# The second piece of the first batch's keys and values asked for on ScalarE's queue

## The chip, the core and the metric

The kernel runs on one core of a Trainium2 chip. The metric is the device time of one launch in microseconds (us). The core's engines are TensorE (PE in the profile; PEld is its weight load), VectorE (DVE), ScalarE (ACT), GpSimd (POOL) and SyncE (SP). SyncE computes nothing here: it issues most of the loads, in the order in which they are written. ScalarE and GpSimd can issue loads and stores too, each on a queue of its own; in the profile SyncE's queue is q1, ScalarE's q10 and GpSimd's q0.

## The reference

Eight batches of eight heads, 576 tokens each, head size 64, 32 slots. The attention goes over slots into which keys and values are summed, and its output goes through a mixture of eight experts, of which each token takes one.

```python
a = exp(phi - max); a = a / (sum + 1e-9)
k_m = einsum('bhsm,bhsd->bhmd', a, k)          # keys and values summed into 32 slots
v_m = einsum('bhsm,bhsd->bhmd', a, v)
attn = softmax(q @ k_m.T / sqrt(64))
x = (attn @ v_m)                               # as 4608 tokens of 512 features
idx = argmax(norm(x) @ norm(emb).T / tau)      # the token's expert
out = gate * (relu(x @ w1[idx]) @ w2[idx])
```

## The kernel before

The eight batches are worked one after the other. For each, the kernel picks one expert, loads that expert's w1 and w2 and computes the whole batch with it; tokens that chose another are noted in flags and worked by a branch at the end if there are any. For the first batch the expert is picked early, from the summed values of the slots, before the attention is done (`summed`, `guess`, `pick`).

The order of every engine's instructions is the order in which the code is written, since the kernel asks for a manual schedule. Waits are put in by semaphores. A load that is issued has landed when its semaphore is full.

The start of the kernel, which the change touches, goes like this. Filler products (`warm`) run on TensorE while nothing else is there. SyncE issues phi of batch 0 in two pieces (tile `ex`), then `load_kv(0)`: keys and values of 512 tokens in two pieces of 1024 KB, `kx[0]` and `kx[1]`, with those of the last 64 tokens (`kl`, 256 KB) between them. Then comes half of q (`qt`). ScalarE issues two small loads for the router (`em`, `tv`), and runs one small exp, which loads its table. The softmax of phi (`softmax`, `largest`), its transposes (`turn`, `tails`) and the sums into slots (`slots`, tiles `acc0t` and `acc0m`) follow. `slots` is called three times for batch 0: with `kx[0]`, then with `kl`, then with `kx[1]`, with three filler products (`hot`) after each of the first two. Behind it stand the scaled sums (`ks`), the keys (`tk`), the pick of the expert, and, on SyncE, the load of the pick's number and the loads of w1 (`load_w1`, in two halves for this batch).

The second batch's keys and values go into the same tiles: `load_kv(1, (0,))` and two calls of `load_piece`, each of which waits until the products that read the tile before are done. The second batch's `slots` runs in five parts, and before the last of them TensorE multiplies the first batch's values with the first half of w1 (`project`, tile `pg`). From the products `ph` on (`first`) TensorE's work is one long row.

Of the kernel before, what the change touches and what calls it, by code (L numbers as in the profile page):

```python
# [307 lines left out]
class Kernel:  # L308
# [156 lines left out]
    def load_kv(self, b, ks=range(2)):  # L465
        if 1 < b < B:
            for g in range(NG):
                to, x = self.kl[64 * g : 64 * g + 64], self.kvt[b, :, 4 * g : 4 * g + 4]
                self.nc.sync.dma_start(to, x)
        if b < B:  # L470
            for k in ks:
                self.nc.sync.dma_start(self.kx[k], self.kv[b, :, 2 * k : 2 * k + 2])
                if b < 2 and not k:
                    x = self.kvt[b].rearrange("t (g j) d -> (t g) (j d)", g=NG)
                    self.nc.sync.dma_start(self.kl.rearrange("p j d -> p (j d)"), x)
# [634 lines left out]
@with_exitstack  # L1110
def moe_linformer(ctx, tc, phiT, qT, kv, kvt, emb, tau, w1, w2, out):
    k = Kernel(ctx, tc, phiT, qT, kv, kvt, emb, tau, w1, w2, out)
    ctx.enter_context(tc.manual_schedule(engines={ET.PE, ET.DVE, ET.Activation, ET.SP, ET.Pool}))


    k.eights()
    k.warm(11)
    k.warm(5, hot=k.mm([P, 64], "cool", 0))
    k.load_phi(0)
    k.load_kv(0)  # L1120
    k.load_q(0, (0,))
    k.load_router()
    k.consts()
    accs = [k.ps.tile([P, 2 * D], F32, tag=f"{n}3", name=f"acc0{n}", bufs=1) for n in "tm"]
    for vT in k.vT:
        k.nc.vector.memset(vT, 0.0)
    router = k.router()
    for g in range(NG):
        k.largest(0, g)
        k.softmax(0, (g,))  # L1130
    for g in range(NG):
        k.turn(0, g)
        if not g:
            next(router)
        k.warm(4 if g else 8, hot=k.mm([P, 256], f"half{g}", 0))
    k.tails(0)
    k.shares(0)
    next(router)
    k.load_phi(1, (0,))
    k.load_q(0, (1,))  # L1140
    k.load_phi(1, (1,))
    t = Tokens(k, 0, k.pt)
    for ks in ((0, 1), (4,), (2, 3)):
        k.slots(0, accs, ks=ks, first=0 in ks, last=3 in ks)
        if 3 not in ks:
            k.warm(3, hot=k.mm([P, 128], f"hot{ks[0]}", 0))
    k.scale(0)
    next(router, None)
    k.warm(2, hot=k.mm([P, 128], "hot2", 0))
    k.load_kv(1, (0,))  # L1150
    k.load_piece(1, 2)
    k.keys(0)
    t.summed()
    k.again()
    values = k.values(0, copy=k.nc.scalar.copy, room=lambda *a: k.mm(*a, 3))
    all, tr, te = slice(0, BL), [k.mm([P, S - 64], f"tr0_{g}", g) for g in range(NG)], [k.mm([P, 64], "te0_0", 2)]
    k.score(0, tr, 64, S, (0,))
    t.guess()
    k.score(0, te, 0, 64, (0,))
    next(values)  # L1160
    t.fill((0,), slice(2, BL), tr)
    e = t.pick()
    t.fill((0,), slice(0, 2), te)
    list(values)
    k.load_w1(e, 0)
    k.load_piece(1, 3)
    k.load_w1(e, 1)
    k.load_q(1, (0,))
    tl = [k.pt([P, D + E], f"tl0_{g}") for g in range(NG)]
    k.squares(0, tl)  # L1170
    k.score(0, tr, 64, S, (1,))
    te.append(k.pt([P, 64], "te0_1"))
    k.score(0, te, 0, 64, (1,))
    k.products(0, copy=True)
    work = [t.weigh((g,), all, None if g else k.nc.gpsimd) for g in range(NG)]
    next(work[0])
    for g in range(NG):
        k.largest(1, g)
    next(work[0])
    t.fill((1,), slice(2, BL), tr)  # L1180
    t.fill((1,), slice(0, 2), te)
    k.softmax(1, (0,))
    list(work[0])
    k.softmax(1, (1,))
    k.warm(12, hot=k.mm([P, 256], "warm0", 3))
    k.turn(1, 0)
    for _ in range(2):
        next(work[1])
    k.warm(9, hot=k.mm([P, 128], "warm1", 3))
    k.turn(1, 1)  # L1190
    list(work[1])
    k.tails(1)
    k.shares(1, v=k.nc.gpsimd, invert=False)
    project = k.project(0, k.vT[0], apart=True)
    accs = [accs[0], k.mm([P, 2 * D], "acc1", 3)]
    for ks in ((0,), (1,), (4,), (2,), (3,)):
        if 3 in ks:
            next(project)
        k.slots(1, accs, ks=ks, first=0 in ks, last=3 in ks)
    next(project)  # L1200
    t.divide(range(NG), all, True, lambda: k.invert(1))
    k.tags, k.turns = 4, 3
    k.scale(1)
    k.again(k.nc.scalar.copy)
    t.turn(range(NG), all)
    for g in range(NG):
        k.part(g, slice(0, HS), k.nc.gpsimd.tensor_copy)
    next(project)

    def between():  # L1210
        k.keys(1, lambda *a: k.mm(*a, 3))
        list(k.values(1, copy=k.nc.scalar.copy, room=lambda *a: k.mm(*a, 2)))

    t.attend(between)
    t.turned(0, 1)
    t.turned(4)
    k.load_w2(e)
    k.load_q(1, (1,))
    k.load_phi(2)
    k.second_part = project  # L1220
    for b in range(B):
        u = Tokens(k, b + 1, k.pt) if b < B - 1 else None
        left = k.batch(b, t, u)
        t = u
    k.rest(*left)
# [29 lines left out]
```

## Time and profile before

| what | us |
| --- | --- |
| median of three runs | 393.88 |
| the three runs | 391.99, 393.88, 394.16 |
| the profiled execution | 392.9 |
| its span, from the first to the last instruction | 391.1 |
| TensorE busy in the span | 382.4 |

The profiled execution is 1.0 us under the median; 1.8 us of it lie outside the span. Times in the rows are microseconds from the span's start. In a row of the timeline the two numbers at the front are start and length, x16 is a count of merged instructions, and the brackets at the end tell how long the engine was idle before, and what ended that. "SPq" and "ACTq" are the issues of loads, not the transfers. A transfer's time is told by the view of the DMA issues, as the time from the issue to the landing.

### The profile page before, as it was taken

What the parts mean: (1) busy time and instruction counts of PE and PEld (TensorE: products, weight loads), DVE (VectorE), ACT (ScalarE), POOL (GpSimd) and SP (SyncE); (2) the same over time, 40 slices, a digit from 0 to 9 for tenths busy, and PEclk for the clock granted to TensorE, in tenths of its full rate; (3) what the DMA queues carried; (4) which work ended last, traced back from release to release, by engine and by line L of the source; (5) the groups of instructions that cost most, each with busy time, mean ns of one, the idle gap of its engine ahead of it and who ended that gap; (6) DMA issues with size and microseconds to landing.
All of it is one profiled execution on the core that took longest, in us unless ns stands there. A gap on an engine that the chain in (4) does not pass through costs nothing. (4 is left out here: it accounts for less than half of the span.)

```text
span 391.1 us, 10317 instructions
## 1 busy us (share of the span) xinstructions
PE 382.4 (98%) x3847; PEld 311.6 (80%) x3847; DVE 243.2 (62%) x800; ACT 213.4 (55%) x665; POOL 190.3 (49%) x234
## 2 busy tenths in 40 slices
PE   8979999999999999999999999999999999999995
PEld 5658878799787978889787987879788897879883
DVE  5668896679673798259862798538861596535000
ACT  5446734778484875666656675657641751145011
POOL 1156940596154932479061951559242871529300
PEclk9999999999999999999999999999999999999999
DMA  8999828993789936995499916996369306890011
GB/s 317 399 370 353 340 63 220 373 398 130 164 272 376 403 80 140 390 392 205 90 286 371 407 38 142 332 393 244 71 180 369 137 2 122 263 370 1 30 54 44
DMA packets 65590, 91.23 MB, mean 233 GB/s; under 512 B 40728, under 2 KB 45336, under 8 KB 63488
## 3 DMA queue, kind: packets, MB, share of 16 engines
q1 hardware_dynamic: 62160, 81.02, 61.2%
q0 software_dynamic: 2688, 8.26, 5.8%
q10 hardware_dynamic: 688, 1.26, 1.2%
q8 instruction: 31, 0.51, 0.5%
q14 instruction: 23, 0.19, 0.1%
HBM read 71.19 MB, written 19.33 MB: 231 GB/s over the span
## 5 line engine op out<-in xcount | busy, mean ns | idle before, releaser
L791 PE MATMUL ph<-aT,gh 128*128 128x288 f32 x512 | 103.1, 296 | 0.0
L831 PE MATMUL py<-wh,hh 128*128 128x512 f32 x256 | 100.9, 394 | 0.0
L831 PE MATMUL py<-wl,hh 128*128 128x512 f32 x256 | 99.8, 390 | 0.0
L831 PE MATMUL py<-wh,hl 128*128 128x512 f32 x256 | 99.7, 389 | 0.0
L756 POOL TENSOR_TENSOR wl<-w2s,wh 128x512 fp32r<-128x512 f32 x64 | 83.2, 1301 | 5.1
L791 PEld LDWEIGHTS ph<-aT,gh 128*128 128x128 f32 x512 | 81.8, 188 | 1.8 <-DVE hl L798 0.8
L791 PE MATMUL ph<-aT,gl 128*128 128x288 f32 x256 | 75.4, 294 | 0.0
L795 ACT ACTIVATE hh<-ph 128x224 fp32r<-128x224 f32 (+1 forms) x128 | 48.8, 388 | 33.5 <-PE ph L791 33.0
L798 DVE SCALAR_TENSOR_TENSOR hl<-ph,hh 128x224 fp32r<-128x224 f32 (+1 forms) x128 | 51.8, 417 | 23.7 <-ACT hh L795 17.2
L997 POOL DMA_DIRECT2D out_dram<-ys x28 | 16.3, 582 | 91.1 <-ACT ys L836 91.0
L836 ACT ACTIVATE ys<-py,gate 128x512 f32<-128x512 f32 (+1 forms) x40 | 25.7, 643 | 63.6 <-PE py L831 33.8
L831 PEld LDWEIGHTS py<-wh,hh 128*128 128x128 f32 x256 | 48.1, 188 | 11.1 <-issue 1.4
L831 PEld LDWEIGHTS py<-wh,hl 128*128 128x128 f32 x256 | 48.1, 188 | 10.2
L831 PEld LDWEIGHTS py<-wl,hh 128*128 128x128 f32 x256 | 48.1, 188 | 9.5
L791 PEld LDWEIGHTS ph<-aT,gl 128*128 128x128 f32 x256 | 48.0, 188 | 0.0
L775 DVE TENSOR_TENSOR gl<-pg,gh 128x512 fp32r<-128x512 f32 x32 | 20.0, 684 | 42.9 <-ACT gh L771 42.9
L755 POOL CAST wh<-w2s 128x512 fp32r<-128x512 f32 x62 | 41.3, 666 | 0.3 <-DMA w2s<-w 0.3
L746 POOL TENSOR_TENSOR aT<-aw,aT 128x576 fp32r<-128x576 f32 (+1 forms) x18 | 23.5, 1320 | 35.0 <-DVE aT L745 29.2
L584 ACT COPY eT<-xt 32x256 f32<-32x256 f32 x80 | 32.3, 404 | 1.4
L820 PE MATMUL py<-w2s,h 128*64 128x256 f32 x256 | 29.4, 382 | 0.0
L656 ACT COPY kv<-kt 32x64 f32<-32x64 f32 x96 | 23.3, 243 | 6.3 <-DVE kt L646 5.1
L820 PEld LDWEIGHTS py<-w2s,h 128*64 128x64 f32 x256 | 17.7, 137 | 10.7 <-DVE aw L102 2.1
(184 smaller groups left out, 471.6 us busy)
## 6 DMA issues: line engine op xcount, KB each, us to landing
kx<-kv SPq DMA_DIRECT2D x15, 1024.0 KB, 11.8
w2s<-w SPq DMA_DIRECT2D x28, 512.0 KB, 9.9
w1s<-w SPq DMA_DIRECT2D x28, 512.0 KB, 6.6
qt<-qT SPq DMA_DIRECT2D x14, 576.0 KB, 9.7
out_dram<-ys POOLq DMA_DIRECT2D x28, 256.0 KB, 6.5
ad<-aw SPq DMA_DIRECT2D x8, 576.0 KB, 11.5
td<-x SPq DMA_DIRECT2D x56, 72.0 KB, 2.3
ea<-td SPq DMA_DIRECT2D x7, 512.0 KB, 4.4
```

Of the source, the lines that this page charges most:

```text
L584: nc.scalar.copy(eT[to, :8, m].rearrange("p (g k) m -> p g k m", g=NG), xt[at, :, q : BL - 2 : 4])
L656: nc.scalar.copy(y, self.kt[32 * l : 32 * l + 32, g, h + 2 * i :: 2 - 4 * i])
L746: self.nc.gpsimd.tensor_tensor(out=al, in0=a, in1=ah.bitcast(F32), op=ALU.subtract)
L755: (copy or self.nc.scalar.copy)(h, x)
L756: self.nc.gpsimd.tensor_tensor(out=l, in0=x, in1=h.bitcast(F32), op=ALU.subtract)
L775: nc.vector.tensor_tensor(out=self.gl[:, g, f], in0=ps[g], in1=self.gh[:, g, f].bitcast(F32), op=ALU.subtract)
L791: nc.tensor.matmul(p, lhsT=w[:, g, fs], rhs=x[:, g, to], start=g == 0 and k == 0, stop=g == 1 and k == 2)
L795: nc.scalar.activation(self.hh[:, f, at], q, AF.Relu)
L798: nc.vector.scalar_tensor_tensor(out=self.hl[:, f, at], in0=q, scalar=0.0, in1=self.hh[:, f, at].bitcast(F32), op0=ALU.max, op1=ALU.subtract)
L820: nc.tensor.matmul(p[64 * j : 64 * j + 64], lhsT=self.h4[:, f], rhs=self.w2s[:, f, d * j : d * j + d], start=f == 0, stop=f == 7,)
L831: nc.tensor.matmul(p, lhsT=h[:, f, to], rhs=w[:, f], start=f == 0 and k == 0, stop=f == 7 and k == 2)
L836: nc.scalar.activation(y[:, :d], p, AF.Copy, scale=gate[:, i : i + 1])
```

## The change

`load_kv` for batch 0 is split into two calls. The first asks for `kx[0]` and `kl` on SyncE, as before. The second, which asks for `kx[1]`, is written behind `load_router`, and issues on ScalarE. For the other batches nothing is different.

```diff
         if b < B:
             for k in ks:
-                self.nc.sync.dma_start(self.kx[k], self.kv[b, :, 2 * k : 2 * k + 2])
+                eng = self.nc.scalar if not b and k else self.nc.sync
+                eng.dma_start(self.kx[k], self.kv[b, :, 2 * k : 2 * k + 2])
@@
     k.load_phi(0)
-    k.load_kv(0)
+    k.load_kv(0, (0,))
     k.load_q(0, (0,))
     k.load_router()
+    k.load_kv(0, (1,))
     k.consts()
```

SyncE at the start of the program, before (`kx_70` and `kx_71` are the two pieces, `ex` is phi, `qt` is q):

```order
L460 DMA ex<-phiT 128x576 x2
L472 DMA kx_70<-kv 128x2048
L475 DMA kl<-kvt 128x512
L472 DMA kx_71<-kv 128x2048
L482 DMA qt<-qT 128x1152
L460 DMA ex<-phiT 128x576
```

SyncE at the same place with the change:

```order
L460 DMA ex<-phiT 128x576 x2
L473 DMA kx_70<-kv 128x2048
L476 DMA kl<-kvt 128x512
L483 DMA qt<-qT 128x1152
L460 DMA ex<-phiT 128x576
```

The issue of `kx_71` is gone from between `kl` and `qt`; the rest of SyncE's row is as it was.

ScalarE at the start of the program, before:

```order
L400 DMA sT<-emb 8x512
L402 DMA tv<-tau 8x1
L403 ACT_TABLE_LOAD
L403 ACTIVATE e_131<-ones 128x1
L524 ACTIVATE ex,sm_158<-ex,nm_157 128x576 x2
L551 COPY eT<-te_0_166 128x512
```

ScalarE at the same place with the change:

```order
L400 DMA sT<-emb 8x512
L402 DMA tv<-tau 8x1
L403 ACT_TABLE_LOAD
L403 ACTIVATE e_130<-ones 128x1
L473 DMA kx_71<-kv 128x2048
L525 ACTIVATE ex,sm_158<-ex,nm_157 128x576 x2
L552 COPY eT<-te_0_166 128x512
```

The issue of `kx_71` now stands behind the small exp and ahead of the exp of phi. On TensorE, VectorE and GpSimd the order is the same as before.

## Rows read from the trace of the kernel before

**Rows 1.** The page's totals: busy us, share of the span, instructions.

```profile
PE 382.4 (98%) x3847; PEld 311.6 (80%) x3847; DVE 243.2 (62%) x800; ACT 213.4 (55%) x665; POOL 190.3 (49%) x234
```

**Rows 2.** Stages: us, each engine's busy us (count), clock, DMA share, GB/s.

```profile
20.00:30.00 10.00, 7.76 (x188) 5.00 (x187) 6.86 (x19) 4.52 (x14) 5.32 (x11) 1.00 1.01 372
30.00:40.00 10.00, 10.00 (x85) 8.82 (x83) 7.79 (x34) 6.84 (x17) 6.73 (x8) 1.00 1.04 343
```

**Rows 3.** Timeline, TensorE, 22 to 25 us: start, length, line, tiles, [idle, releaser].

```profile
22.44 0.42 PE L607 MATMUL acc<-kx,eT 128*32 128x128 f32 x8
...
24.11 1.09 PE L766 MATMUL pg<-w1s,kv 64*32 64x512 f32 x16 [1.25 <-DMA w1s<-w]
```

**Rows 4.** Timeline, issues on SyncE, 1.6 to 17 us.

```profile
1.63 0.42 SPq L472 DMA_DIRECT2D kx<-kv  x1
...
2.10 0.43 SPq L475 DMA_DIRECT2D kl<-kvt  x1
...
2.57 0.43 SPq L472 DMA_DIRECT2D kx<-kv  x1
...
9.38 0.33 SPq L472 DMA_DIRECT2D kx<-kv  x1
...
10.26 0.33 SPq L475 DMA_DIRECT2D kl<-kvt  x1
...
16.62 0.72 SPq L494 DMA_DIRECT2D w1s<-w  x1
```

**Rows 5.** DMA issues at 0.70, 1.63, 2.10, 2.57, 10.26, 16.62: KB, us to landing.

```profile
ex<-phiT SPq DMA_DIRECT2D x1, 288.0 KB, 3.0
...
kx<-kv SPq DMA_DIRECT2D x1, 1024.0 KB, 6.0
...
kl<-kvt SPq DMA_DIRECT2D x1, 256.0 KB, 6.2
...
kx<-kv SPq DMA_DIRECT2D x1, 1024.0 KB, 8.2
...
kl<-kvt SPq DMA_DIRECT2D x1, 256.0 KB, 9.0
...
w1s<-w SPq DMA_DIRECT2D x1, 1024.0 KB, 7.4
```

**Rows 6.** DMA view of 4 to 11 us: packets, MB, mean rate.

```profile
DMA packets 582, 2.88 MB, mean 412 GB/s; under 512 B 64, under 2 KB 64, under 8 KB 338
```

**Rows 7.** Waits of SyncE's queue to 40 us: total us, times, longest.

```profile
SPq L460 <- PE te L550: 3.2, 2, 2.7
```

**Rows 8.** Timeline, ScalarE, 2.9 to 5 us.

```profile
2.95 0.20 ACT L403 ACTIVATE e<-ones 128x1 f32<-128x1 bf16 x1
...
4.48 0.78 ACT L524 ACTIVATE ex<-ex,nm 128x576 f32<-128x576 f32 x1 [1.33 <-DVE nm L509]
```

**Rows 9.** DMA view of 100 to 101 us: packets by queue; issues, us to landing.

```profile
q10 hardware_dynamic: 101, 0.22, 71.2%
q1 hardware_dynamic: 51, 0.00, 3.8%
...
td<-x SPq DMA_DIRECT2D x3, 72.0 KB, 5.6
```

**Rows 10.** Timeline, TensorE, 9.5 to 11.5 us.

```profile
9.52 0.30 PE L607 MATMUL acc0t<-kl,kt 128*32 128x128 f32 x1
...
10.11 0.34 PE L444 MATMUL hot<-ones 128*128 128x128 bf16 x3
10.83 0.64 PE L607 MATMUL acc0t<-kx,eT 128*32 128x128 f32 x16 [0.38 <-DMA kx<-kv]
```

**Rows 11.** Timeline, VectorE's last transpose into aw, and the second group's products.

```profile
25.41 0.20 DVE L102 STREAM_TRANSPOSE aw<-x 128x64 f32<-128x64 f32 x1
...
28.46 0.86 PE L135 MATMUL po<-vv,aw 64*64 64x72 f32 x40
```

**Rows 12.** Stage from 7 to 8 us, columns as in rows 2.

```profile
7.00:8.00 1.00, 1.00 (x11) 0.95 (x10) 0.41 (x4) 0.89 (x3) 0.00 (x0) 1.00 1.12 469
```

## The prediction

> **What bounds the kernel now.** I read the totals first, then the stages, then the waits at the start. TensorE is busy 98% of the span [rows 1]. From 30 us it is busy in 10.00 of 10.00 us, while the stage from 20 to 30 us shows 7.76 of 10.00 [rows 2]. So a change in the first 30 us reaches the end only if it moves the point at which the continuous work begins. The reader should see in those two rows that there is no idle time later that could hide or give back anything.
>
> What holds that point is one wait. The last product of the second batch's keys and values before it ends at 22.44 + 0.42 = 22.86 us, and the products with w1 begin at 24.11 us after 1.25 us of idle TensorE, released by the landing of w1 [rows 3]. The first half of w1 is asked for at 16.62 us [rows 4] and lands 7.4 us later, at 24.02 us [rows 5]. That wait is the transfers' own rate and not the moment of asking. A phi piece of 288 KB that stood first in the queue took 3.0 us to land [rows 5]; the other 736 KB of a 1024 KB piece at the 412 GB/s of the stretch from 4 to 11 us [rows 6] take 1.83 us more. So w1 with nothing ahead of it would land in about 4.8 us, an estimate, against 7.4 measured. Some 2.6 us of it is queueing behind what was asked for before. The queue on SyncE has been full since the start; from 4 to 11 us it moves 2.88 MB at that rate.
>
> **The change, part by part.** Three loads of the first batch's keys and values stand in a row on SyncE: kx (first piece, 1024 KB) at 1.63, kl (256 KB) at 2.10, kx (second piece, 1024 KB, the one that moves) at 2.57 us [rows 4]; a q piece follows. By the landings [rows 5] they end at 7.63, 8.30 and 10.77 us. So kl has 0.67 us of the stream to itself and the second piece 2.47 us.
>
> *Removed from SyncE:* one issue, of about 0.45 us. The q piece goes out that much earlier. The next issue on SyncE waits up to 2.7 us for TensorE's transposes anyway [rows 7], so this is worth nothing.
>
> *Added on ScalarE:* one issue behind the two small router loads, the table load and the first exp, which ends at 2.95 + 0.20 = 3.15 us. The next instruction on ScalarE is the exp of phi at 4.48 us, after 1.33 us of idle time that waits for VectorE's maximum [rows 8]. An issue on SyncE took 0.42 to 0.43 us at this point [rows 4]; I take the same for ScalarE, which fits three times between 3.15 and 4.48 us. Without that gap it would cost its own length. It has no wait of its own. The piece is asked for 3.15 - 2.57 = 0.58 us later than before, but it no longer stands behind kl.
>
> *The order in which the loads land.* This is the term that decides. With two queues the second piece need not wait for kl, and kl may wait for it. The trace has one place where both queues hold work, phi of a later batch on q10 with the small stores of another on q1. Between 100 and 101 us q10 moved 101 packets and q1 51 small ones, although stores on SyncE's queue took 5.6 us to land there [rows 9]. So ScalarE's queue is served while SyncE's has a backlog, and takes the larger part. I therefore take the whole second piece to go between the first piece and kl: it lands at 7.63 + 2.47 = 10.10 us, and kl at 10.77 us instead of 8.30 us.
>
> TensorE uses them in the order first piece, kl, second piece. The products with kl start at 9.52 us [rows 10], and now wait until just after 10.77 us; TensorE began 0.06 us after the second piece's landing before (10.83 against 10.77), so 10.83 us. From the start of kl's products to the end of the filler products behind them are 10.11 + 0.34 - 9.52 = 0.93 us. The products with the second piece start at 10.83 + 0.93 = 11.76 us, where they started at 10.83 us after 0.38 us of waiting for that piece [rows 10]. The wait of 0.38 us goes and one of some 1.3 us takes its place, on kl. The chain behind it moves by **+0.93 us**.
>
> The bounds of that term: if kl is not held up at all, the chain moves by -0.38 us, the old wait. If the second piece delays the first piece by its whole 2.47 us as well, the chain moves by 2.47 - 0.38 = +2.09 us. I keep +0.93, since a piece of 1024 KB that is asked for 1.5 us after the first has most of that one ahead of it.
>
> The Trainium skill (DMA: Bandwidth & Descriptors, Queues, rings and completion order) says that each DMA engine goes round between the queues that have work and drains one whole packet of descriptors from one before it turns to the next. By that rule kl would wait for all of the second piece's share on its engine, which is the +0.93 case; the packet counts above do not contradict it, and the sum at the end would be the same.
>
> *Who is behind the chain.* Each follower is checked at +0.93 us:
> - TensorE's own last product before w1 ends at 22.86 + 0.93 = 23.79 us, still 0.32 us before 24.11 us. The wait for w1 shrinks and its end stays.
> - The issue of w1 on SyncE goes from 16.62 to 17.55 us, since the picked expert is known later. With 4.8 us unqueued it could land at 22.4 us, so the queue still decides, at 24.02 us. The bytes ahead of it are the same as before, only over two queues.
> - VectorE's last transpose into aw ends at 25.41 + 0.20 = 25.61 us and now at 26.54 us; the products that read that group run from 28.46 us [rows 11]. There is 1.9 us of room.
> - The later loads on SyncE stand behind w1 in a full queue.
>
> **The sum:** 0.58 us later asked for, -0.38 us of one wait, +1.31 us of another, -1.25 us of room in front of w1: nothing is left at 24.11 us. The end moves by **0.0 us**, with +0.84 us (2.09 - 1.25) at the upper bound of the order.
>
> **Rivals.**
>
> *Slower: ScalarE's queue gets nothing while SyncE's has work.* Then SyncE's queue runs through everything that does not depend on the second piece: q and phi pieces, and the next kx and kl, asked for at 9.38 and 10.26 us [rows 4]. That kl landed 9.0 us after its issue [rows 5], at 19.26 us. Without the 2.47 us of the second piece ahead of it that is 16.79 us, and the second piece would land at 19.26 us, 8.49 us late. Less the 1.25 us of room the end moves by +7.2 us, to about 400.7 us. It decides from a delay of 1.25 us on, and costs 2 us from 3.25 us on. Against it stand the 101 packets [rows 9]. Chance 0.04.
>
> *Slightly slower: the clock.* The new wait of some 1.3 us before kl is idle TensorE. If the granted clock fell to 1.2 GHz in it, 1 us of products behind it would take 2 us, and 1 - 0.32 = +0.7 us would reach the end, 394.2 us, for each such us. Against it: in the stage from 20 to 30 us TensorE stands idle for 1.25 us in one piece [rows 3], and the granted clock of that stage is 1.00 throughout [rows 2], the 2.4 GHz level. Chance 0.05, together with the upper bound of the order.
>
> *Faster: two queues move the same bytes faster.* The best single us of the start, 7 to 8, ran at 469 GB/s [rows 12]. If 2.88 MB went at that rate in place of 412, they would take 6.14 us in place of 6.99; w1 lands 0.85 us earlier, and TensorE is ready for it if the chain moved by less than 0.4 us. The end moves by at most -0.85 us, 392.7 us. Against it: the engines' share there is already full with one queue, 1.12 in that us. Chance 0.07. The Trainium skill (DMA: Bandwidth & Descriptors, Issuing engines are not separate DMA queues) states that loads from several issuing engines run on the same DMA engines and interleave; by it this rival falls away.
>
> **How the numbers follow.** The profiled execution took 392.9 us, 391.1 of it the span; the median of the three runs is 393.88 us (391.99 to 394.16). With 0.0 us the profiled time stays 392.9 us. For the median I take 393.5 us, between the profiled execution and the median, since three runs that are 2.2 us apart place it no better. The forecast has a chance of 0.84, the three rivals 0.16. A measurement of this kernel can tell about 0.5% from no change, 2.0 us. The order's bounds (0 to +0.84 us), the faster rival (-0.85 us) and the spread of the runs (about 1 us either way) give 391.8 to 395.2 us; only the starved queue lies outside. All cases but that one are within 0.5%; what the runs' own scatter may put outside makes 0.04 on the faster side and 0.02 beside the 0.04 on the slower one: 0.04, 0.90, 0.06.
>
> **What would show it.** In the changed kernel's trace: the second kx piece issued on ScalarE's queue near 3.15 us and the exp of phi still at 4.5 us; the wait for the second piece before its products gone; a wait of about 1.3 us before the products with kl, with kl landing near 10.8 us; the issue of w1 near 17.5 us; and TensorE's products with w1 at 24.1 us all the same, with a wait in front of them that is shorter by about 0.9 us. If kl still lands near 8.3 us, the order is wrong and the chain is early, but 24.1 us should hold. If the products with w1 start elsewhere than 23.9 to 24.5 us, the forecast's last step is wrong.

## The result and the profile after

The changed kernel takes 397.21 us (median of 22 runs, 393.63 to 399.59) against 393.88 us (22 runs, 391.21 to 397.28): a ratio of 1.0081, interval 1.0054 to 1.0108. The ratio leaves out the slowest run, 399.59 us, which lies over 1.5% above the fastest of this kernel. The change is slower by 3.3 us, where 393.5 us and no change were forecast; the time lies 2.0 us above the range.

The profiled execution of after took 393.91 us, with a span of 392.1 us: only 1.0 us more than before's, though the medians are 3.3 us apart. Each run lists its mean granted clock, and the gap goes with it. In 12 of the 22 runs the clock is 0.992 or less, and they took 397.0 to 399.6 us; the other ten have 0.993 or more, and took 393.6 to 396.0 us. The medians of the two groups are 398.5 and 395.0 us. The profiled one is of the second kind. So there are two losses to find: about 1 us that the second group has too, and some 3.5 us more that over half of the executions have.

The page's totals, the answer to [rows 1], and the stages, the answer to [rows 2] (us, each engine's busy us with counts, clock, DMA share, GB/s):

```profile
PE 382.3 (98%) x3847; PEld 311.8 (80%) x3847; DVE 242.7 (62%) x800; ACT 212.9 (54%) x665; POOL 190.1 (48%) x234
```

```profile
20.00:30.00 10.00, 8.11 (x196) 5.34 (x193) 6.87 (x15) 5.12 (x15) 5.75 (x11) 1.00 1.01 370
30.00:40.00 10.00, 9.79 (x88) 8.53 (x82) 8.13 (x39) 6.58 (x17) 6.05 (x8) 1.00 1.04 360
```

The work is the same. The stage from 30 us is no longer full from its start: the long row of products begins later.

The start of after, timeline of all engines (start, length, engine, line, operation), the answer to [rows 4, 8]:

```profile
1.63 0.42 SPq L473 DMA_DIRECT2D kx<-kv  x1
1.67 1.28 ACT L403 ACT_TABLE_LOAD   x1 [1.67 <-PEq L1249]
...
1.73 0.36 ACTq L473 DMA_DIRECT2D kx<-kv  x1
...
2.09 0.43 SPq L476 DMA_DIRECT2D kl<-kvt  x1
...
2.96 0.20 ACT L403 ACTIVATE e<-ones 128x1 f32<-128x1 bf16 x1
```

ScalarE asks for the second piece at 1.73 us, 0.10 us after SyncE asked for the first, while ScalarE's own table load is still running and its small exp has not begun. The prediction had 3.15 us. So both 1024 KB pieces are with the transfer engines at once. When they landed (view of the DMA issues, from 2.0 us; KB, us from issue to landing), the answer to [rows 5], and who moved what from 4 to 8 us (packets, MB, share of 16 engines):

```profile
kx<-kv SPq DMA_DIRECT2D x1, 1024.0 KB, 7.8
kx<-kv ACTq DMA_DIRECT2D x1, 1024.0 KB, 8.1
...
kl<-kvt SPq DMA_DIRECT2D x1, 256.0 KB, 8.3
```

```profile
q1 hardware_dynamic: 137, 0.95, 56.3%
q10 hardware_dynamic: 93, 0.76, 44.9%
```

The two queues share the engines almost evenly, 0.95 to 0.76 MB. The first piece lands at 1.63 + 7.8 = 9.4 us instead of 7.6, the second at 9.8 instead of 10.8, and kl at 10.4 instead of 8.3 us. What TensorE makes of it (timeline; the brackets give the idle time before and what ended it), the answer to [rows 3, 10]:

```profile
9.55 0.65 PE L608 MATMUL acc0t<-kx,eT 128*32 128x128 f32 x16 [1.47 <-DMA kx<-kv]
...
10.84 0.30 PE L608 MATMUL acc0t<-kl,kt 128*32 128x128 f32 x1
...
11.70 0.65 PE L608 MATMUL acc0t<-kx,eT 128*32 128x128 f32 x16
...
20.39 0.66 PE L551 MATMUL te<-ident,ex 128*128 128x128 f32 x4
...
23.65 1.09 PE L767 MATMUL pg<-w1s,kv 64*32 64x512 f32 x16
...
25.47 1.04 PE L135 MATMUL po<-vv,aw 64*64 64x72 f32 x28
28.24 0.47 PE L135 MATMUL po<-vv,aw 64*64 64x72 f32 x12 [1.73 <-issue]
...
30.93 0.51 PE L792 MATMUL ph<-aT,gh 128*128 128x288 f32 x2
```

TensorE waits 1.47 us for the *first* piece, and for neither of the other two. The chain is 11.70 - 10.83 = 0.87 us late at the second piece. The products with w1 (`pg`) start at 23.65 us, without a wait and 0.46 us *earlier* than before; w1 was asked for at 17.48 us and landed sooner (view of the DMA issues):

```profile
w1s<-w SPq DMA_DIRECT2D x1, 1024.0 KB, 5.5
```

And yet the long row (`ph`) starts at 30.93 us, 0.77 us later than before's. Before's first products and its long row:

```profile
8.23 0.65 PE L607 MATMUL acc0t<-kx,eT 128*32 128x128 f32 x16
...
30.16 0.51 PE L791 MATMUL ph<-aT,gh 128*128 128x288 f32 x2
```

Between `pg` and `ph` of after stand 1.73 us in which TensorE waits inside one group of products (`po`), not for a load and not for another engine: "issue" means that nothing the profile shows held it. Before had the same wait at the same product, but a short one (its own timeline):

```profile
27.48 0.47 PE L135 MATMUL po<-vv,aw 64*64 64x72 f32 x12 [0.51 <-issue]
```

At 27.48 + 0.76 = 28.24 us the 0.8 us of the late chain are all there, and they stay to the end. What TensorE may wait for here stands in the DMA view: a queue named "instruction" (q8) moves one packet of 16 KB among the loads, in after between 25.5 and 26 us:

```profile
q1 hardware_dynamic: 98, 0.20, 102.9%
q8 instruction: 1, 0.02, 12.4%
```

By the trace's records it starts at 25.90 us, and at 25.12 us in before; TensorE goes on 2.34 and 2.36 us behind it. By the queue's name these are instructions. Whether TensorE waits for them, and what the clock does, the runs had to tell.

### The profile page after: what moved, and what is told of

Read it like the earlier page. It is cut to its first block, busy times and chain, and to the rows that moved or that the text cites. A ratio compares the mean times of both kernels' runs of the same rounds, so it can differ in the third digit from the quotient of the medians.

```text
span 392.1 us, 10317 instructions
## 1 busy us (share of the span) xinstructions
PE 382.3 (98%) x3847; PEld 311.8 (80%) x3847; DVE 242.7 (62%) x800; ACT 212.9 (54%) x665; POOL 190.1 (48%) x234
## 5 line engine op out<-in xcount | busy, mean ns | idle before, releaser
L832 PEld LDWEIGHTS py<-wh,hh 128*128 128x128 f32 x256 | 48.1, 188 | 11.1 <-issue 1.4
## 6 DMA issues: line engine op xcount, KB each, us to landing
w2s<-w SPq DMA_DIRECT2D x28, 512.0 KB, 10.5
```

Of the source, the lines that this page charges most:

```text
L832: nc.tensor.matmul(p, lhsT=h[:, f, to], rhs=w[:, f], start=f == 0 and k == 0, stop=f == 7 and k == 2)
```

## The experiments

**After, once more.** No edit; the trace of a second execution, since the first had kept its clock.

> The changed kernel once more, for a second trace. Its 22 times lie in two groups, 10 from 393.6 to 396.0 us and 12 from 397.0 to 399.6 us, and the trace in hand (span 392.1 us) is of the lower group. Theory C (clock): in the upper group TensorE's granted clock falls to 1.2 GHz in the new idle time before the first piece's products (1.47 us, 8.1 to 9.55 us) or in the one at 26.3 to 28.2 us; a trace of that group shows a granted clock under 1.00 in some stretch of the first 40 us and a span near 396 us. Theory D (transfers): the upper group shows clock 1.00 and a later landing of some load, with the first long row of products starting some 4 us later than 30.9 us.

398.46 us, span 396.5 us, mean clock 0.988. TensorE's timeline:

```profile
11.29 0.69 PE L608 MATMUL acc0t<-kx,eT 128*32 128x128 f32 x16 [3.01 <-DMA kx<-kv]
...
23.58 0.65 PE L551 MATMUL te<-ident,ex 128*128 128x128 f32 x4
...
26.84 1.09 PE L767 MATMUL pg<-w1s,kv 64*32 64x512 f32 x16
...
31.61 0.47 PE L135 MATMUL po<-vv,aw 64*64 64x72 f32 x12 [1.91 <-issue]
...
35.48 0.59 PE L792 MATMUL ph<-aT,gh 128*128 128x288 f32 x2
```

Its stages, columns as above, the clock third from the end:

```profile
8.00:12.00 4.00, 0.99 (x27) 0.79 (x29) 2.10 (x12) 0.62 (x2) 0.00 (x0) 0.97 1.01 405
12.00:16.00 4.00, 4.00 (x72) 2.60 (x64) 0.35 (x1) 0.00 (x0) 0.00 (x0) 0.60 0.95 331
...
28.00:32.00 4.00, 2.05 (x56) 1.45 (x56) 2.72 (x6) 1.86 (x5) 3.04 (x5) 1.00 1.05 414
32.00:36.00 4.00, 4.00 (x57) 3.52 (x54) 1.21 (x7) 1.75 (x7) 0.00 (x0) 0.57 1.03 408
```

The first piece landed 9.5 us after its issue, at 11.1 us. TensorE stood idle for 3.01 us, and behind that the granted clock fell to the 1.2 GHz level: from 11.75 to 15.17 us it is 0.50 throughout. It fell again, 32.23 to 35.65 us, behind the 1.91 us of waiting for instructions. Both stretches are full of work, so each costs 3.42 / 2 = 1.7 us there. The long row starts at 35.48 us, 5.3 us later than before's, and the span is 5.4 us longer. So an execution with a low clock has the same fault, here with a later landing, and the clock on top: the two falls are 3.4 us of the 4.4 us by which this span is longer than the first execution's. By the same arithmetic, as an estimate, one such fall takes 0.004 off a run's mean clock. The end of the span, up to its last 2.7 us, stands at 0.50 in most traces, before's too, and takes off up to 0.003. A mean of 0.988 to 0.991 then tells of two early falls, and one of 0.992 to 0.996 can hold one.

**The new idle time filled, too short.** After, with six filler products of 512 columns behind the transposes, in front of the first piece's products; three wider fillers instead of nine further on keep the count of instructions.

```diff
     k.tails(0)
+    k.warm(6, hot=k.mm([P, 512], "fill", 0))
@@
-    k.warm(9, hot=k.mm([P, 128], "warm1", 3))
+    k.warm(3, hot=k.mm([P, 384], "warm1", 3))
```

> The changed kernel, with six filler products of 512 columns more in front of the first piece's products, in the time in which TensorE waits for that piece (and the nine filler products of 128 columns later made three of 384, so that the number of TensorE's instructions from there on is nearly that of before). Theory C: TensorE idles at most 0.3 us before the first piece, the clock stays, the upper group of times is gone, and the median is 394 to 395 us, some 0.2% above before. Theory D, or a clock that falls in the idle time at 26 to 28 us: two groups as in the changed kernel, median near 397 us.

A miss: 397.06 us median of 12 runs against 394.70 us of before, which was run again beside this and the next two kernels (23 runs), ratio 1.0064 (1.0031 to 1.0098), and 5 of 12 runs at a clock of 0.992 or less. The piece landed at 11.2 us, later than the profiled execution of after had shown, and the fillers ended at 9.6 us:

```profile
8.15 1.46 PE L444 MATMUL fill<-ones 128*128 128x512 bf16 x6
11.32 0.64 PE L608 MATMUL acc0t<-kx,eT 128*32 128x128 f32 x16 [1.72 <-DMA kx<-kv]
```

With 1.72 us still idle it said nothing on the clock. It did show that 9.4 us was near the early end of the landing: in the seven traces here with both pieces asked for together it lies between 9.2 and 11.6 us.

**The second piece asked for later.** After, but ScalarE issues it behind the first exp of phi, which waits for VectorE's maximum.

```diff
     k.load_router()
-    k.load_kv(0, (1,))
@@
         k.softmax(0, (g,))
+        if not g:
+            k.load_kv(0, (1,))
```

> The second piece stays on ScalarE's queue, but is asked for behind the first exp of phi, at some 4.5 us in place of 1.73 us. Theory Q (the piece shares the engines with the first piece from 4 us on and holds it up by 1.8 us): the first piece lands before 8.4 us, TensorE waits less than 0.3 us for it, the expert is picked within 0.3 us of before (w1 asked for at 16.3 to 16.9 us) and the time is that of before within 0.3%. Rival (the second queue costs as such): slower by 0.5% or more as in the changed kernel.

395.82 us against 394.70 us of before, ratio 1.0025 (1.0001 to 1.0049): two thirds of the loss are gone. ScalarE's timeline, then TensorE's:

```profile
4.43 0.77 ACT L525 ACTIVATE ex<-ex,nm 128x576 f32<-128x576 f32 x1 [1.27 <-DVE nm L510]
4.44 0.36 ACTq L473 DMA_DIRECT2D kx<-kv  x1
```

```profile
8.80 0.64 PE L608 MATMUL acc0t<-kx,eT 128*32 128x128 f32 x16
...
10.95 0.27 PE L608 MATMUL acc0t<-kl,kt 128*32 128x128 f32 x1 [0.80 <-DMA kl<-kvt]
...
12.81 0.65 PE L608 MATMUL acc0t<-kx,eT 128*32 128x128 f32 x16 [0.92 <-DMA kx<-kv]
```

Here the issue went out at 4.44 us, with the exp that had waited for its operand. The wait for the first piece is gone, as expected, though the piece landed at 8.7 us, not before 8.4, and w1 was asked for at 18.60 us, not by 16.9. In its place stand a wait on kl, 0.80 us, for which the prediction had looked, and one on the second piece, 0.92 us, for which it had not: the pieces landed in the order first piece, kl (10.8 us), second piece (12.8 us). With the first piece no longer held up by the second, the change costs less. The clock fell in this execution too, behind the wait in `po`:

```profile
29.21 0.47 PE L135 MATMUL po<-vv,aw 64*64 64x72 f32 x12 [1.20 <-issue]
```

```profile
29.00:33.00 4.00, 3.79 (x61) 3.23 (x62) 1.01 (x6) 1.20 (x5) 0.14 (x1) 0.58 1.04 414
```

**The late landing alone, on one queue.** Before, all loads on SyncE; six of the eight heads of the second piece are asked for ahead of the first piece, the other two behind kl.

```diff
-    k.load_kv(0)
+    k.nc.sync.dma_start(k.kx[1][:, :, :6], k.kv[0, :, 2:4, :6])
+    k.load_kv(0, (0,))
+    k.nc.sync.dma_start(k.kx[1][:, :, 6:], k.kv[0, :, 2:4, 6:])
```

> The kernel before with everything on SyncE's queue, but three quarters of the second piece asked for ahead of the first, the rest behind kl. By the bytes the first piece lands near 7.63 + 1.85 = 9.5 us and the second as before. Theory Q with theory C: what costs is that the first piece lands late and not the second queue, so the waits, the two groups of times and the median (some 0.8% above before) are those of the changed kernel. Rival (the second queue costs as such): the time of before within 0.3%.

397.31 us against 394.70 us of before, ratio 1.0088 (1.0053 to 1.0122), the same as after's. The piece landed 8.2 us behind its issue at 2.10 us:

```profile
10.40 0.64 PE L607 MATMUL acc0t<-kx,eT 128*32 128x128 f32 x16 [1.71 <-DMA kx<-kv]
```

So the whole loss is there with every load on one queue: a first piece that lands late is enough for it, and ScalarE's queue is not needed. The profiled execution is the one of seven that escaped (393.79 us); three of the others had a clock of 0.992 or less, three 0.996, and all six took 397.1 to 398.9 us. What held the three with 0.996 no trace shows.

**Fillers until the piece is there.** After, with 13 fillers in place of six; others are made wider and fewer, so that the count of TensorE's instructions stays.

```diff
     k.tails(0)
+    k.warm(13, hot=k.mm([P, 512], "fill", 0))
@@
-    k.warm(2, hot=k.mm([P, 128], "hot2", 0))
+    k.warm(1, hot=k.mm([P, 256], "hot2", 0))
@@
-    k.warm(12, hot=k.mm([P, 256], "warm0", 3))
+    k.warm(6, hot=k.mm([P, 512], "warm0", 3))
@@
-    k.warm(9, hot=k.mm([P, 128], "warm1", 3))
+    k.warm(3, hot=k.mm([P, 384], "warm1", 3))
```

> The changed kernel with thirteen filler products of 512 columns in front of the first piece's products (2.8 us; six left 1.72 us idle, since the first piece landed at 11.2 us), and later fillers made fewer and wider so that the number of TensorE's instructions from the second batch's transposes on is as before. Theory C (clock, first fall): TensorE does not idle before the first piece's products; the granted clock does not fall there; the first piece still lands at 9.4 to 11.3 us and the expert is picked as late as in the changed kernel. Of the 3.3 us the clock's share goes: median 0.3 to 0.6% above before in place of 0.8%, with mean clocks of 0.995 and up in most runs, and falls only behind the second idle time. Rival (the late landing alone costs it, the clock only goes with it): median 0.8% above before.

395.66 us against 393.58 us of before, which was run once more beside this and the next two kernels (29 runs), ratio 1.0050 (1.0022 to 1.0078). One of 12 runs has a clock of 0.992 or less, where after had 12 of 22. After itself was not run beside these kernels, and here before's clock fell less too: at 0.996 or less are 1 of before's 29 runs here and 6 of its 23 runs beside the kernels above, against 3 of 12 with the fillers and 18 of 22 for after. So a part of the difference can have come with the time at which they were run. The timeline:

```profile
8.20 2.97 PE L444 MATMUL fill<-ones 128*128 128x512 bf16 x13
11.10 0.64 PE L608 MATMUL acc0t<-kx,eT 128*32 128x128 f32 x16
...
30.03 0.47 PE L135 MATMUL po<-vv,aw 64*64 64x72 f32 x12 [1.75 <-issue]
...
32.71 0.51 PE L792 MATMUL ph<-aT,gh 128*128 128x288 f32 x2
```

No idle time stands before the first piece's products, and the falls of the clock are nearly gone. What is left is the late chain: the long row starts 32.71 - 30.16 = 2.55 us later than before's. Some of that is the fillers' own, since the piece landed at 10.5 us and they ran until 11.1 us. The intervals of this ratio and after's overlap; the counts of low clocks carry the reading, not the ratios.

**Fewer instructions on TensorE.** Before, with 27 filler products fewer and the others wider, so that they take the same time (each is two instructions, a weight load and a product, so 54 fewer). If the wait at `po` comes with a fixed number of instructions, it must leave that place.

```diff
-    k.warm(5, hot=k.mm([P, 64], "cool", 0))
+    k.warm(1, hot=k.mm([P, 320], "cool", 0))
@@
-        k.warm(4 if g else 8, hot=k.mm([P, 256], f"half{g}", 0))
+        k.warm(2 if g else 4, hot=k.mm([P, 512], f"half{g}", 0))
@@
-            k.warm(3, hot=k.mm([P, 128], f"hot{ks[0]}", 0))
+            k.warm(1, hot=k.mm([P, 384], f"hot{ks[0]}", 0))
```

(`hot2`, `warm0` and `warm1` are changed as in the run above.)

> The kernel before with the same filler columns in 54 instructions fewer (wider and fewer fillers, the first eleven untouched). Theory F (the idle time before the first group's po products, 0.51 us with no releaser in the kernel before and 1.73 us with the change, is TensorE waiting for its own instructions, fetched on queue q8 behind the loads' data, after it has passed a point some 7.5 us earlier): the idle time moves 54 instructions on, out of the first group's po products into or behind the keys' transposes, and 7.3 to 7.6 us behind the moment at which TensorE is at the shifted point; first ph product 0.2 to 0.6 us earlier than 30.16 us. Rival (something at that place holds the po products): the idle time stays in front of the same twelve po products.

It left. All 40 products stand in one row:

```profile
11.81 0.64 PE L607 MATMUL acc0t<-kx,eT 128*32 128x128 f32 x16 [0.85 <-DMA kx<-kv]
...
25.04 1.09 PE L766 MATMUL pg<-w1s,kv 64*32 64x512 f32 x16 [1.20 <-DMA w1s<-w]
...
26.93 1.11 PE L135 MATMUL po<-vv,aw 64*64 64x72 f32 x40
...
28.55 1.00 PE L135 MATMUL po<-vv,aw 64*64 64x72 f32 x40
...
30.25 0.51 PE L791 MATMUL ph<-aT,gh 128*128 128x288 f32 x2
```

The loads of this profiled execution came late: the second piece's products begin 1.0 us later than before's, and `pg` 0.9 us, still behind a wait of 1.20 us. At `ph` only 0.09 us of that are left, because the wait inside `po` is gone; so it had cost some 0.8 us in before. That `ph` would come earlier than before's was a miss. The wait did come back where it was expected, but small: in the second group of `po` the even row of products breaks at the eleventh and twelfth, at 28.79 us. That is 26 and 27 products on, 2.4 us behind this trace's q8 packet at 26.42 us, and the group takes 1.00 us in place of 0.86. But the kernel is slower, 395.15 us against 393.58 us of before, ratio 1.0039 (1.0015 to 1.0062). The view of TensorE's waits over the whole span has a new line, which the timeline puts at 106.26 us:

```profile
PE acc L607 <- issue: 0.6, 1, 0.6
```

Some of the later fetches had moved with the instructions, to places where nothing hides them. Followed product by product against before, the row is 0.09 us late up to 105 us, 1.02 us from 107 us on, 1.33 from 243, 2.09 from 349 and 2.34 from 369 us on. The first two steps come 2.4 to 2.5 us behind a q8 packet (103.72 and 239.87 us); at the third, TensorE's weight loads wait 0.6 us for w1; the fourth I have not followed.

**Both.** After with the 13 fillers and with all fillers wider and fewer (28 instructions less on TensorE than after).

> The changed kernel with the thirteen fillers before the first piece's products and the wider and fewer fillers of the previous run everywhere else (28 instructions fewer in all). Theories C and F: the first idle time is gone, the second is shorter or moved by 28 instructions; mean clocks of 0.995 and up in nearly all runs, median within 0.4% of before. Rival: median 0.8% above before whatever is done to TensorE's idle times.

395.07 us against 393.58 us of before, ratio 1.0035 (1.0014 to 1.0057). No run of 12 has a clock under 0.997, and they lie within 394.5 to 395.9 us. The wait for instructions moved on by 28 instructions, from the middle of `po` to `tv`:

```profile
30.45 0.44 PE L668 MATMUL tv<-ident,ks 128*128 128x128 f32 x2 [1.31 <-issue]
```

**What the instructions wait for.** Over the traces so far that wait had one pattern. From the second batch's second row of transposes `te` to the q8 packet, and from that to TensorE's going on (us; the two kernels whose instructions moved have no row):

| kernel | te | q8 packet | later by | po goes on | later by |
| --- | --- | --- | --- | --- | --- |
| before | 19.53 | 25.12 | 5.6 | 27.48 | 2.4 |
| after | 20.39 | 25.90 | 5.5 | 28.24 | 2.3 |
| after, again | 23.58 | 29.23 | 5.6 | 31.61 | 2.4 |
| six fillers | 22.16 | 27.64 | 5.5 | 30.14 | 2.5 |
| asked for later | 21.50 | 26.90 | 5.4 | 29.21 | 2.3 |
| on one queue | 21.25 | 25.61 | 4.4 | 27.89 | 2.3 |
| 13 fillers | 22.16 | 27.66 | 5.5 | 30.03 | 2.4 |

So in six of the seven TensorE goes on 7.7 to 8.0 us after `te`, that is after its own progress; on one queue it is 6.6 us. Two runs, of one execution each, ask what the 5.5 us are. The first adds a load of 512 KB on ScalarE's queue near 18 us (a part of batch 7 that nothing reads):

```diff
     k.softmax(1, (0,))
+    k.nc.scalar.dma_start(k.ea[:, :4], k.kv[7, :, 0].rearrange("p (c h) d -> p c (h d)", c=4))
```

> The kernel after, and one more load of 512 KB (keys and values of batch 7 into a tile that is free at that time), asked for on ScalarE's queue behind the exps of the second batch's phi, near 19 us. It reads TensorE's idle time in front of the products po, where the view of waits names only the engine's own issue. Measured so far: the one 16 KB packet of the instruction queue (q8) moves 5.4 to 5.7 us after the start of the second batch's second row of transposes te, and TensorE goes on 2.3 to 2.5 us after that packet, in six of seven traces. If the instructions queue behind load data on the transfer engines, that distance grows by about what half of 512 KB to all of it takes at 400 GB/s, 0.6 to 1.3 us: the packet moves 6.1 to 7.0 us after te. If the distance is a fixed time of the fetch itself, it stays 5.4 to 5.7 us.

The packet moved at 25.10 us, 4.9 us behind `te` at 20.16 us. Neither number came: not later, as queueing behind all data would have it, and not the fixed 5.4 to 5.7 us. The wait itself could not show here, since TensorE stood until 27.24 us for a later piece of keys and values. The second run holds loads back instead:

```diff
-    k.load_w1(e, 1)
-    k.load_q(1, (0,))
@@
     k.scale(1)
+    gate = k.dp.tile([P, NG, 3 * D], F32, name="gate")
+    k.nc.sync.dma_start(gate, k.ks)
+    k.load_w1(e, 1)
+    k.load_q(1, (0,))
```

> The kernel after, with the loads of w1's second half, q and w2 held back on SyncE behind a small store of the second batch's scaled sums, that is until about 27 us in place of 18 to 22 us. From about 24 us on, when w1's first half and the last piece of keys and values have landed, nothing else is in the queue. If the instructions queue behind load data, the packet of q8 moves at most 4.5 us after te, not 5.4 to 5.7, and the idle time before po (1.73 us in the kernel after) falls under 0.8 us. If the distance is a fixed time of the fetch, the packet still moves 5.4 to 5.7 us after te and the idle time stays 1.5 us or more. The total time says nothing here: w1's second half and w2 arrive late, and TensorE must wait for them behind 31 us, by some 5 us or more.

The packet moved at 24.79 us, 3.1 us behind `te` at 21.73 us, and the wait for instructions is gone; the 40 products stand in one row, held only by VectorE:

```profile
21.73 0.65 PE L551 MATMUL te<-ident,ex 128*128 128x128 f32 x4
...
26.81 1.18 PE L135 MATMUL po<-vv,aw 64*64 64x72 f32 x40 [0.16 <-DVE aw L102]
...
31.43 0.69 PE L668 MATMUL tv<-ident,ks 128*128 128x128 f32 x2 [3.08 <-ACT ks L662]
```

The total, 399.02 us, says nothing on this, but not because of late weights, as had been expected. ScalarE's copy into `ks` (L662) waits 3.36 us for the store that holds the loads back, TensorE waits 3.08 us for that copy, and the clock is at 0.50 for 6.83 us from 30.14 us on. With less load data behind w1's first half on SyncE's queue, the packet comes 2.4 us sooner after `te`, just behind the last load data, which moved at 24.74 us. So the wait is no fixed time, and it was shorter with less load data in the queue; that the instructions queue behind load data is what this one execution suggests. How the length follows from the queues stays open: the extra load on the other queue did not lengthen it.

## Why the prediction was wrong

- **The moment of asking** (3.15 us): failed. The prediction put ScalarE's issue behind the instructions that stand ahead of it. It went out at 1.73 us, beside the table load, so the piece was asked for 0.84 us earlier than before, not 0.58 us later. The issue on SyncE that went away cost nothing, as said, and the exp of phi stayed at 4.48 us.
- **The order of landing**: failed with it. The first piece was taken to land at 7.63 us all the same, because the second was asked for 1.5 us behind it. Asked for 0.10 us behind it, the second took nearly half of the engines, and the first landed at 9.2 to 11.6 us in the seven traces. The chain's +0.87 us in the profiled execution looks like the forecast +0.93 us, but it comes by another wait, and the likeness is luck; in the other traced execution of after the delay was 3.1 us at the first piece already (11.29 against 8.23 us), more than the bound of 2.09 us that was kept for the second piece delaying the first. What makes 9.4 us of one execution 11.1 us of the next I have not found.
- **The 1.25 us of room in front of w1**: failed, and with it the 0.0 us of the sum, by 0.8 us in the profiled execution. The room was there: w1, asked for at 17.48 us (17.55 forecast), landed in 5.5 us, and `pg` began 0.46 us early, outside the 23.9 to 24.5 us that the prediction had set as the sign of its last step. It was worth nothing, because 3 us further on TensorE waits for its own instructions, and that moment moves with TensorE's progress at 20 us, that is with the late chain, not with w1. The row for it, 27.48 us with 0.51 us of idle time, was in the trace of before, 3 us behind the point at which the prediction took the delay to be absorbed. The stage from 20 to 30 us had 10.00 - 7.76 = 2.24 us of idle time, of which the prediction read 1.25 us; the list of followers went by loads and engines and left this wait out. (The 0.58 us in the line of the sum is no part of it: the +0.93 us is 1.31 - 0.38.) And w1 itself need not stay where it lands: in the trace with 54 instructions fewer, whose chain was 1.0 us late at the second piece, its issue went from 16.62 to 17.60 us and its landing moved by the same 1.0 us, 7.4 us behind the issue both times, so that the wait in front of `pg` did not shrink. There the row was caught up only where the wait for instructions had been.
- **The clock**: a rival at 0.05, and the larger part of the loss in over half of the executions. Its price held: 3.42 us at 1.2 GHz cost 1.7 us, twice in the execution looked at. Its place did not: it looked at the wait before kl, and the falls came behind the waits before the first piece and in `po`. Its chance was wrong. The evidence against it was one execution in which 1.25 us of idle time left the clock at 1.00. After has 12 of 22 executions at 0.992 or less; before, in its runs beside the experiments, 2 of 52. Which idle time brings a fall the traces leave open: 3.01 and 1.91 us in one execution and 1.20 us in another were followed by one, while 1.47 and 1.73 us in the profiled execution of after, and 1.72 us with six fillers, were not.
- **The other rivals**: the starved queue fell (93 packets on q10 beside 137 on q1). The faster one fell too: from 4 to 11 us after moved 2.94 MB at 419 GB/s, against 2.88 MB at 412 in before, not at the rival's 469. That w1 landed 1.0 us earlier all the same I have not followed.
- **The range**: its upper end was worked from +0.84 us, the chain's bound less the room, and about 1 us of scatter. With the bound broken and the room worthless, nothing held it at 395.2 us.

## What to carry to other kernels

Before moving a load to another queue, find out who else is in the transfer engines at that moment: two large loads asked for together landed together here (9.4 and 9.8 us), so the one that is needed first should be alone in front. A wait with time to spare is only room if no later gate depends on the engine's earlier position; look in the trace for idle times that end with "issue", since here TensorE's own instructions came among the loads. And where a change puts a microsecond or two of idle time on TensorE, weigh the clock by many executions, not by the one that was profiled.

## What the runs showed of the hardware

- **A load asked for on ScalarE passes work that is running, not work that waits for another engine.** It went out at 1.73 us beside a table load of 1.28 us and ahead of an exp at 2.96 us; behind an exp that waited for VectorE it went out at 4.44 us, with the exp's start. The Trainium skill (Advanced Engine Details and Errata, Sequencer Loop) says that the sequencer puts engine instructions into a queue, where they wait for their semaphores, and reads on. The first case agrees; by that wording the waiting exp should not have held the issue back either, and there the measurement, 4.44 us, decides.
- **Two queues share about evenly** when both hold large loads: 0.95 MB against 0.76 MB in 4 us, in the other execution of after 0.85 against 0.75. The rule cited in the prediction, that an engine drains a whole packet of descriptors before it turns to the other queue (the Trainium skill, DMA: Bandwidth & Descriptors, Queues, rings and completion order), agrees with the trace in so far as both queues were served through the same 4 us. The reading made of it there, that kl would wait for the whole second piece and the first piece for none of it, it does not bear out: both pieces and kl ended within 1 us of each other (9.4, 9.8 and 10.4 us).
- **TensorE's instructions come in 16 KB packets while it runs**, among load data, as the two shifts by 54 and by 28 instructions show: 3.1 to 5.6 us from TensorE's passing a fixed point to the packet, and 2.3 to 2.5 us more until it goes on. Taking instructions out moves these points, and may put one where it shows: 0.6 us at 106 us, in a kernel that did the same work.
